# A gated linear attention feeding a gated MLP on one core: a shorter weight conversion, a third engine for v's copies, and a new table of due times

## The chip, the cores and the metric

The kernel runs on one core of a Trainium2 chip. The metric is device time in microseconds, the median over several executions of the program. One core has five engines with a queue of instructions each: TensorE (PE in the profile, with its weight loads as PEld), VectorE (DVE), ScalarE (ACT), GpSimd (POOL) and SyncE (SP), which here issues all DMAs.

## The reference

```python
# attention: batch 4, heads 8, sequence 768, head size 48
f = 1.0 / (1.0 + np.exp(-f_logit))
for t in range(S):
    state = f[:, :, t, :, None] * state + einsum('bhd,bhe->bhde', k[:, :, t], v[:, :, t])
    y[:, :, t] = einsum('bhd,bhde->bhe', q[:, :, t], state)
x = y.transpose(0, 2, 1, 3).reshape(B, S, H * D)          # 4 x 768 x 384
# MLP with a spatial gate: d_ff 1024, halves of 512
h = gelu_tanh(x @ w_in)
u, v = h[..., :512], h[..., 512:]
v_n = (v - mean(v)) / sqrt(var(v) + 1e-06) * g_ln
v_s = einsum('ts,bsd->btd', w_sg, v_n) + b_sg[None, :, None]
return x + (u * v_s) @ w_out
```

q, k, v, the gates, `w_sg` and the output are float32. `w_in` and `w_out` are float64: the kernel gets them as pairs of 32-bit words and turns them into float32 on the chip.

## The kernel before, in words

**Tiles.** Tokens go in 24 tiles n of 128 (six to a batch; tiles 0 to 5 are batch 0). Attention works on chunks of 64 tokens, two to a tile. The MLP works on groups g of three tiles, with four slices ft of 128 features.

**Two-word products.** The MLP's matmuls run on pairs "hi" and "lo" in a rounded float32 format, three matmuls to a product (`mm3`, L691), so every operand is split: ScalarE writes hi as a cast, VectorE writes lo as the difference.

**Steps.** The program is a list of named steps. For tile n:

- `f`, `k`, `q`, `v`: loads on SP. `w{n}.0`, `w{n}.1`: copies of half of v's heads to the other 64 partitions.
- `e`, `l` (exp, ln on ScalarE), then `cum` (matmul), then `up`, `dn` (exp on ScalarE), `mq`, `mk` (products); for tiles from 6 on, `lh`, `ll` split the logarithm ahead of `cum`.
- `tr` and `tc` turn k and q on PE for tiles 0 to 5. For the others it goes over DRAM: `tt` (VectorE transposes 32x32 blocks), `to` and `ti` (DMA out to `kq_d` and back into `raw`), `tc` (copy).
- `su` (scores and state updates, 128 small matmuls), `ms` (mask), `sa`, `sm` (state), `y` (128 small matmuls), `ty` (ScalarE), `jy` (VectorE), `xT` (three PE transposes), `xh`, `xl` (split).
- `hv` (MLP's v half), `gv` (gelu on ScalarE), `ns`, `nd`, `nq`, `nr`, `nh`, `nl` (the norm; `nr` on POOL).
- For group g: `hu`, `gu` (u half), `sg` (spatial gate, 18 matmuls each, after all six `nl` of the batch), `sb`, `sm_`, `sh`, `sl` (gate and split), `po` for each tile (projection), `re` (residual), `out` (store).

The weights go through `ld`, `wa` to `wf`: eight pieces `in0` to `in7` of w_in (0 to 3 for `hu`, 4 to 7 for `hv`) and four `out0` to `out3` of w_out; `ldsg`, `wT`, `wh`, `wl` do w_sg. In the kernel before a piece takes one ScalarE pass (`wa`), then `wb`, `wp`, `wq`, `wr`, `wc` on VectorE, `wd` and `wf` on VectorE or POOL, `we` on ScalarE.

**The order** is neither the source's nor the hardware's. `Plan` runs a list scheduling over the steps with costs from the table `T` (microseconds by engine) and `W` (SP's issue and the wire), due times worked back from the PE units, four PSUM banks, and rings of buffers (`gg` 5, `u` 8, `tmp` 3, `f` 4 and so on). Where `T` names several engines for a step, the planner picks one. `MOVES` shifts the due time of single steps and pins some to an engine. What comes out is written to the engines' queues as it stands, and each engine works its queue in order. Before 45 us of plan time, `warm` puts matmuls on zeros (L1044) wherever the plan leaves PE free. ScalarE keeps one table of functions: exp and ln are in one, gelu in the other, and each change between them is an ACT_TABLE_LOAD (L318).

A second path for gates out of range stands behind the main one and does not run with these inputs.

Of the kernel before, what the change touches and what calls it, by code (L numbers as in the profile page):

```python
# [66 lines left out]
wbin0:388.1 wdin0:-42.7:POOL wcin1:371.6 wrin3:343.8 wcin3:-99.1 wdin3:305.4:DVE wdin4:86.5 wfin4:224.6:DVE wrin5:88.5  # L67
wbin6:70.5 wfin6:-0.5:POOL wbin7:342.5 wrin7:222.5 wfin7:136.9:POOL ldout0:43.3 wfout0:-139 ldout1:444.3
wdout1:136.6:POOL wfout2:61.6 waout3:53.5 wbout3:-15.3 wT0.0:91.5 wh0.1:-323.2 wh1.0:110.6 ldsg2:2 wT2.1:74.4
wT3.0:32.3 wT3.1:232.8 wh4.0:7.4 ldsg5:32.4 mk0:0:DVE gv0:144.9 sm1.0:199.8:DVE xl1:61.2 v2:144.4 mk2:12 sa2.0:-2.5  # L70
sm2.0:340.9:DVE hu0.0:375.7 sm_0.0:-69.3:POOL sh0.0:-10.7 gu0.1:-79.4 sh0.1:-351.3 sm_0.2:73.7:DVE sg0.3:8.6
sm_0.3:-17.5:POOL po2:3.4 q3:27.8 w3.0:279.8:POOL w3.1:134.8 mq3:18.2:POOL di3:0:ACT tr3:227.2 sa3.0:169.8
sm3.0:-36.7:POOL xT3:264 w4.0:31.8:DVE sm4.0:0:POOL sm4.1:-12.4:POOL di5:-1.7:ACT sa5.0:15.5 nq5:-64.4 sg1.0:60.2
hu1.1:-126.3 gu1.1:75.2 gu1.2:304 sg1.2:-16.5 sm_1.3:-21.7:POOL sh1.3:13.3 sl1.3:-78.5 w6.1:493.6 ll6:0:DVE
tt6.0:229.6 tc6.0:23:ACT jy6:-75.7 xh6:-10.7 hv6:871.9 w7.0:-989.6:DVE w7.1:12.5:DVE ll7:0:DVE up7:128.7 mq7:-20.5:DVE
tt7.0:-318.4 re7:0.4 l8:57.9 cum8:383.5 mq8:-15.5:POOL mk8:-82.7:POOL ti8.3:80.5 tc8.1:6.9:DVE w9.0:0.2 mq9:70.4:POOL
su9:-124.4 xh9:304.7 k10:3.4 w10.1:-0.7:POOL e10:94.9 ll10:0:POOL mq10:-57.5:POOL mk10:99.2:DVE ti10.0:58.9 y10:78.5
k11:-124.5 lh11:66.2:ACT ll11:-2.8 mq11:2.7:POOL sg3.0:97.1 sg3.1:1.3 gu3.3:322.4 sg3.3:226.2 lh12:1.3:DVE up12:-79.1
tc12.0:-7.4:ACT nh12:-0.2 nl12:70.3 w13.0:75.3 w13.1:15.3 lh13:-59.7:ACT tc13.0:-224.1:ACT tc13.1:28.3 sm13.0:132.2
nq13:46.6 v14:14.3 tc14.1:-0.4:DVE hu4.1:161 sm_4.1:0:POOL f15:1.4 lh15:97.8:DVE ll15:29:POOL mq15:26.2:DVE  # L80
tc15.0:-201.2:DVE sm15.1:0.4:POOL f16:46.8 cum16:-214.9 ti16.2:-27.6 sm16.0:14 lh17:-144.9:DVE tc17.1:0:DVE sg5.1:84.7
up18:-24.4 mq18:-24.2:POOL tt18.1:-11 tc18.0:2.9 hv18:176.5 ll19:44.9 mq19:61.5 mk19:63.2:POOL sm19.1:-76 ll20:3.7
tc20.1:75.1:ACT hu6.1:185.8 sm_6.2:-119.2 sg6.3:95.4 sm_6.3:62.9 k21:-26.5 lh21:279.1:ACT tc21.0:-3.3 w22.0:-80.9
w22.1:148.4:POOL lh22:0:DVE tc22.0:36:DVE tc22.1:0.9 sm22.0:-85.9:DVE sm22.1:200.1:DVE w23.1:24.1:POOL ll23:81.9:POOL
mk23:85.3 sm23.0:0:POOL
# [210 lines left out]
def gla_moe_kernel(ctx: ExitStack, tc: tile.TileContext, q, k, v, f, w_in, g_ln, w_sg, b_sg, w_out, cst, out):  # L296
    nc = tc.nc
# [97 lines left out]
    def w_abs(key):  # L395

        w = staged[key].rearrange("p (n x) -> p n x", x=2)
        t = [buf("u", [P, E], U32, j) for j in range(2)]
        nc.scalar.activation(t[0].bitcast(F32), w[:, :, 1].bitcast(F32), AF.Abs)
        w_tmp[key] = (w, *t)  # L400

    def w_scale(key):
        _, a, _ = w_tmp[key]
        nc.vector.tensor_scalar(a.bitcast(F32), a.bitcast(F32), F32_LEAST, 2.0**16, op0=ALU.max, op1=ALU.mult)

    def w_shift(key):
        _, a, _ = w_tmp[key]
        nc.vector.tensor_scalar(a, a, 4, 1, op0=ALU.logical_shift_left, op1=ALU.logical_shift_right)
# [752 lines left out]
```

## Time and profile before

| | |
|---|---|
| median of 3 runs | 380.57 us (379.48 to 382.3) |
| the profiled execution | 379.31 us; its span, first to last instruction, 377.5 us |
| PE busy | 359.7 us, 95% of the span |
| DVE, ACT, POOL busy | 250.7, 244.7, 51.9 us |
| matmuls on zeros (L1044) | 14.8 us of PE |
| ACT_TABLE_LOAD | 36 (35 on L318, one on L300), 1283 ns each |
| mean granted PE clock | 0.992 of full |

PE's busy time holds the matmuls on zeros. Steps named above are found in the profile by line and tile: `hv`, `hu`, `sg`, `po` are all L691 and differ in their operands, `su` is L619 and L624, `y` L667, `xT` L696, `wb` L404, `wp` L408, v's copies and others L325.

### The profile page before, as it was taken

To read this page: it belongs to the slowest core of one execution; us is meant where nothing else is said; L and a number is where in the kernel's file an instruction comes from. 1 tells how busy PE (TensorE), PEld (TensorE's weight loads), DVE (VectorE), ACT (ScalarE), POOL (GpSimd) and SP (SyncE) were. 2 spreads that over 40 slices of the span, in tenths; PEclk is the share of its full clock that TensorE was granted. 3 is DMA by queue.
4 is the path that set the end of the run, shared out by engine and by line. 5 is a ranking of instruction groups with operands and counts; after the bars stand their busy time and mean duration, and the time that the engine had idled before them with its cause. 6 is when DMAs were issued, how large, how long until landed. Compare 5 with 4: busy or idle time off the path is not lost.

```text
span 377.5 us, 11316 instructions
## 1 busy us (share of the span) xinstructions
PE 359.7 (95%) x4662; PEld 324.7 (86%) x4662; DVE 250.7 (66%) x588; ACT 244.7 (65%) x507; POOL 51.9 (14%) x95
## 2 busy tenths in 40 slices
PE   8998999899999998799999999999999999999993
...
PEclk9999999999999999899999999999999999999998
...
GB/s 165 245 205 231 207 209 244 175 86 128 44 168 148 131 170 175 161 195 179 135 160 116 0 65 172 169 190 112 36 43 119 104 55 25 2 0 0 3 63 69
DMA packets 145998, 46.30 MB, mean 123 GB/s; under 512 B 117524, under 2 KB 144532, under 8 KB 145940
## 3 DMA queue, kind: packets, MB, share of 16 engines
...
HBM read 33.64 MB, written 11.85 MB: 121 GB/s over the span
## 4 chain that ended last, share of the span: by engine, by line
PE 55%; ACT 18%; DMA 10%; DVE 8%; SPq 3%; issue 3%; POOL 1%; ACTq 0%
PE ps_b L691 40%; ACT L318 5%; PE ps_b L1044 4%; PE ps_y L667 3%; DMA raw<-kq_d 3%; ACT vg L320 2%; ACT sk L325 2%; SPq L599 2%; DMA f<-in_f_logit_dram 2%; ACT f L320 2%; ACT vg L733 2%; ACT vh L746 2%; PE ps_s L619 2%; PE ps_b L521 1%; DMA kq<-in_q_dram 1%
## 5 line engine op out<-in xcount | busy, mean ns | idle before, releaser
L691 PE MATMUL ps_b<-w_sg_hi,vh 128*128 128x384 f32 x192 | 65.7, 342 | 0.0
L691 PE MATMUL ps_b<-w_sg_lo,vh 128*128 128x384 f32 x192 | 64.8, 338 | 0.0
L691 PE MATMUL ps_b<-w_sg_hi,vh_lo 128*128 128x384 f32 x192 | 64.8, 338 | 0.0
L691 PE MATMUL ps_b<-w_out_hi,gg 128*128 128x384 f32 x174 | 48.1, 339 | 0.4 <-ACT f L320 0.4
L318 ACT ACT_TABLE_LOAD x35 | 44.9, 1283 | 0.6
L794 ACT CAST gg<-tmp 128x384 fp32r<-128x384 f32 x29 | 14.8, 511 | 43.8 <-DVE tmp L783 37.7
L691 PEld LDWEIGHTS ps_b<-w_sg_hi,vh 128*128 128x128 f32 x192 | 36.0, 188 | 0.6 <-DVE w_sg_lo L939 0.2
L691 PEld LDWEIGHTS ps_b<-w_sg_lo,vh 128*128 128x128 f32 x192 | 36.1, 188 | 0.1
L691 PEld LDWEIGHTS ps_b<-w_sg_hi,vh_lo 128*128 128x128 f32 x192 | 36.0, 188 | 0.0
L320 ACT ACTIVATE f<-f 128x384 f32<-128x384 f32 x48 | 24.6, 522 | 12.9 <-DMA f<-in_f_logit_dram 12.6
L691 PEld LDWEIGHTS ps_b<-w_out_hi,gg 128*128 128x128 f32 x174 | 31.7, 188 | 1.0 <-ACT f L320 0.8
L691 PE MATMUL ps_b<-xTh,w_in_hi 128*128 128x384 f32 x84 | 29.3, 348 | 1.8 <-ACT vg L320 1.7
L778 DVE SCALAR_TENSOR_TENSOR tmp<-ps_b,cols,b_bc 128x384 f32<-128x384 f32 x32 | 19.6, 612 | 17.0 <-PE ps_b L691 17.0
L667 PEld LDWEIGHTS ps_y<-vs,st 64*64 64x64 f32 x768 | 24.7, 134 | 6.5 <-issue 5.2
L751 DVE SCALAR_TENSOR_TENSOR vh_lo<-vg,vg_rs,vh 128x512 fp32r<-128x512 f32 x24 | 18.0, 749 | 17.4 <-ACT vh L746 17.3
L691 PE MATMUL ps_b<-w_out_lo,gg 128*128 128x384 f32 x87 | 29.1, 335 | 0.0
L667 PE MATMUL ps_y<-S,sk 48*64 48x48 f32 x768 | 27.4, 220 | 1.2 <-issue 1.2
L691 PE MATMUL ps_b<-xTl,w_in_hi 128*128 128x384 f32 x84 | 28.4, 338 | 0.0
L691 PE MATMUL ps_b<-xTh,w_in_lo 128*128 128x384 f32 x84 | 28.4, 338 | 0.0
L691 PE MATMUL ps_b<-w_in_hi,xTh 128*128 128x512 f32 x63 | 26.9, 427 | 0.9 <-DVE xTl L716 0.9
L667 PE MATMUL ps_y<-vs,st 64*64 64x48 f32 x768 | 27.7, 220 | 0.0
L619 PE MATMUL ps_s<-sk 48*64 48x64 f32 x768 | 24.1, 231 | 1.9 <-ACT sk L325 1.9
...
## 6 DMA issues: line engine op xcount, KB each, us to landing
...
```

The lines of the kernel that those rows point to most:

```text
L318: nc.scalar.preload_act_table_set(SETS[want])
L320: nc.scalar.activation(dst, src, func, **kw)
L325: (nc.scalar.copy if e == "ACT" else ENG[e].tensor_copy)(dst, src)
L599: ENG[e].dma_start(raw[row : row + r1 - r0].rearrange("d b a t -> d b (a t)"), kq_d[n, :, r0:r1, m].rearrange("b r j y -> r b (j y)"))
L619: nc.tensor.matmul(ps_s[rows(score_rows(c, 2 * p + par)), par, p * C : (p + 1) * C], sk[r, 0, p, c], sk[r, 1, p, c], start=True, stop=True)
L667: nc.tensor.matmul(ps_y[rows(c), half, h * D : (h + 1) * D], a, m, start=start, stop=stop)
L691: nc.tensor.matmul(ps, a, m, start=(j == 0), stop=(j == len(seq) - 1))
L733: nc.scalar.activation(v_raw[n], v_raw[n], AF.Identity, bias=v_st[n][0][:, 0:1])
L751: nc.vector.scalar_tensor_tensor(vl, v_raw.pop(n), rs, vh.bitcast(F32), op0=ALU.mult, op1=ALU.subtract)
L778: nc.vector.scalar_tensor_tensor(t, psum[f"sg{g}.{ft}"][:, :E], g_col[:, ft : ft + 1], b_bc[:, tokens(g)], op0=ALU.mult, op1=ALU.add)
L794: nc.scalar.copy(gt[(g, ft)][0], g_raw[(g, ft)])
L1044: steps = plan.warm(plan.run(), 45.0, lambda k, n: nc.tensor.matmul(ps_b[k][:, : n * P], zeros, zeros[:, None, :].to_broadcast((P, n, P)), ...
```

## The change

**The conversion.** A piece loses one VectorE pass. Before, `wb` clamped and scaled the absolute value and `wp` shifted it left by four and right by one; now the scaling is the `scale` of ScalarE's `wa`, which was an Abs without one, and `wp` shifts left by three alone. `wb` is gone, twelve instructions in all.

**v's copies** may now go on ScalarE too. The plan puts 5 of the 48 there, 6 on POOL and 37 on VectorE; before it was 6 on POOL and 42 on VectorE.

**The table of moves** is another one, found with step times that were disturbed at random. It moves steps on every engine.

```diff
-F32_LEAST = float(np.uint32(0x38100000).view(np.float32))
+EXP_DOWN = 2.0**-112
...
-    ok_e="DVE:0.25", w="DVE:0.267 POOL:0.45", wT=0.25, ...
+    ok_e="DVE:0.25", w="DVE:0.267 POOL:0.45 ACT:0.33", wT=0.25, ...
...
 MOVES = """
-wbin0:388.1 wdin0:-42.7:POOL wcin1:371.6 wrin3:343.8 ...
+cs:-38.3 wain0:-74.5 wdin0:8.6:POOL ldin1:-40.4 wfin1:-79.9:POOL ...
...
-        nc.scalar.activation(t[0].bitcast(F32), w[:, :, 1].bitcast(F32), AF.Abs)
+        nc.scalar.activation(t[0].bitcast(F32), w[:, :, 1].bitcast(F32), AF.Abs, scale=EXP_DOWN)
         w_tmp[key] = (w, *t)
-
-    def w_scale(key):
-        _, a, _ = w_tmp[key]
-        nc.vector.tensor_scalar(a.bitcast(F32), a.bitcast(F32), F32_LEAST, 2.0**16, op0=ALU.max, op1=ALU.mult)
 
     def w_shift(key):
         _, a, _ = w_tmp[key]
-        nc.vector.tensor_scalar(a, a, 4, 1, op0=ALU.logical_shift_left, op1=ALU.logical_shift_right)
+        nc.vector.tensor_scalar(a, a, 3, None, op0=ALU.logical_shift_left)
...
-            op("wb" + s, lambda e, key=key: w_scale(key), T["wb"], ["wa" + s], port=True)
-            op("wp" + s, lambda e, key=key: w_shift(key), T["wp"], ["wb" + s], port=True)
+            op("wp" + s, lambda e, key=key: w_shift(key), T["wp"], ["wa" + s], port=True)
```

**Where steps move.** The lines of the kernel after the change are three or four lower than those of before (L691 becomes L688, L1044 becomes L1040). Three places follow.

The head of SP's queue before (gate logits `f`, the constants `cs`, q and k of tile 0 in `kq_90`, v, then four pieces of w_in):

```order
L480 DMA f<-in_f_logit_dram 128x8x48
L911 DMA cs<-in_consts_dram 128x320
L480 DMA f<-in_f_logit_dram 128x8x48
L483 DMA kq_90<-in_q_dram 128x8x48
L483 DMA kq_90<-in_k_dram 128x8x48
L486 DMA vs_93<-in_v_dram 128x8x48
L483 DMA kq_91<-in_q_dram 128x8x48
L390 DMA gg<-in_moe_w_in_dram 128x3x256 x4
L483 DMA kq_91<-in_k_dram 128x8x48
L480 DMA f<-in_f_logit_dram 128x8x48
```

The same place now:

```order
L382 DMA gg<-in_moe_w_out_dram 128x768
L477 DMA f<-in_f_logit_dram 128x8x48
L908 DMA cs<-in_consts_dram 128x320
L480 DMA kq_90<-in_q_dram 128x8x48
L391 DMA gg<-in_moe_w_in_dram 128x3x256
L480 DMA kq_90<-in_k_dram 128x8x48
L477 DMA f<-in_f_logit_dram 128x8x48
L483 DMA vs_93<-in_v_dram 128x8x48
L480 DMA kq_91<-in_q_dram 128x8x48
L391 DMA gg<-in_moe_w_in_dram 128x3x256
L480 DMA kq_91<-in_k_dram 128x8x48
L391 DMA gg<-in_moe_w_in_dram 128x3x256 x3
```

Two pieces of weights, `out3` and `in1`, have moved ahead of the first tile's operands; they were the 58th and the 29th transfer of the queue before. All that stands behind them up to the third `f` has two transfers of weights more ahead of it.

ScalarE's queue from the table load ahead of the first gelu, `gv0`, before (the gelu writes `vg`; `sk` and `w_sg_hi_80` are copies out of PSUM, `w_in_hi` a split):

```order
L318 ACT_TABLE_LOAD
L320 ACTIVATE vg,vg_mv<-ps_b_69 128x512
L325 COPY sk_96<-ps_b_68 112x512
L325 COPY sk_96<-ps_b_67 112x512
L671 COPY x<-ps_y 128x384
L712 CAST w_sg_hi_80<-ps_b_69 128x3x128
L320 ACTIVATE vg,vg_mv<-ps_b_70 128x512
L938 CAST w_sg_hi_79<-ps_b_67 128x3x128
L325 CAST w_in_hi_75<-u 128x3x128
L733 ACTIVATE vg<-vg,vg_mv 128x512 x2
L738 ACTIVATE vh_lo,vg_mv<-vg 128x512 x2
```

The same place now:

```order
L319 ACT_TABLE_LOAD
L321 ACTIVATE vg,vg_mv<-ps_b_67 128x512
L326 COPY sk_97<-ps_b_70 112x512
L400 ACTIVATE u<-gg 128x384
L730 ACTIVATE vg<-vg,vg_mv 128x512
L326 COPY dec<-ps_b_68 112x4x2
L735 ACTIVATE vh_lo,vg_mv<-vg 128x512
L709 CAST w_sg_hi_80<-ps_b_67 128x3x128
L934 CAST w_sg_hi_79<-ps_b_68 128x3x128
L319 ACT_TABLE_LOAD
L321 ACTIVATE eb_103<-ps_b_69 128x8x48
L668 COPY x<-ps_y 128x384
```

`gv0` has come forward, with fewer steps ahead of it, and the table goes back to exp (for `eb`, step `up5`) eight instructions later; before, the second gelu came without a table load in between. Over the whole main path the table loads become 44, from 36.

PE's queue between `y10` and `y11` (tiles 10 and 11, L667 here, L664 after) before: the end of `y10`, `cum15` (two matmuls on lh and ll), `xT10`, and the start of `y11`:

```order
L667 MATMUL ps_y<-vs_94,st 64x48
L667 MATMUL ps_y<-S_100,sk_96 64x48
L524 MATMUL ps_b_68<-lh,cum 128x384
L525 MATMUL ps_b_68<-ll,cum 128x384
L696 MATMUL ps_b_67<-cs,x 128x128 x3
L667 MATMUL ps_y<-vs_95,st 64x48 x2
L667 MATMUL ps_y<-S_101,sk_97 64x48 x3
```

Now `y10` is followed by `su11`, `hu2.3` and `po4`, and then by this: `xT10`, the nine rows of `po5`, `xT9`, the first matmul of `cum15`, with `y11` behind it.

```order
L693 MATMUL ps_b_70<-cs,x 128x128 x3
L688 MATMUL ps_b_69<-w_out_hi,gg 128x384
L688 MATMUL ps_b_69<-w_out_lo,gg 128x384
L688 MATMUL ps_b_69<-w_out_hi,gg 128x384 x2
L688 MATMUL ps_b_69<-w_out_lo,gg 128x384
L688 MATMUL ps_b_69<-w_out_hi,gg 128x384 x2
L688 MATMUL ps_b_69<-w_out_lo,gg 128x384
L688 MATMUL ps_b_69<-w_out_hi,gg 128x384 x2
L688 MATMUL ps_b_69<-w_out_lo,gg 128x384
L688 MATMUL ps_b_69<-w_out_hi,gg 128x384
L693 MATMUL ps_b_67<-cs,x 128x128 x3
L521 MATMUL ps_b_68<-lh,cum 128x384
```

What stood directly behind one another, `y10`, its transposes and `y11`, now has `su11` and three large products in between.

More of the change, by code (lines that the diff above doesn't have):

```diff
@@ L47 @@
     nl="DVE:0.663", gu="ACT:0.38", sb="DVE:0.534", sm_="DVE:0.468 POOL:1.05", sh="ACT:0.402", sl="DVE:0.467", re="DVE:0.467", ok="DVE:1.2",
-    ok_e="DVE:0.25", w="DVE:0.267 POOL:0.45", wT=0.25, cumf=0.72, cum=0.352, do=0.716, tr=0.791, tt="DVE:0.48", zr="POOL:2.2", tr_c="ACT:0.49 DVE:0.46", su=0.83, y=0.905, xT=0.25, hv=2.094, hu=1.584,
+    ok_e="DVE:0.25", w="DVE:0.267 POOL:0.45 ACT:0.33", wT=0.25, cumf=0.72, cum=0.352, do=0.716, tr=0.791, tt="DVE:0.48", zr="POOL:2.2", tr_c="ACT:0.49 DVE:0.46", su=0.83, y=0.905, xT=0.25, hv=2.094, hu=1.584,
     sg=3.167, po=2.084, ok_s=0.12,
@@ L66 @@
 MOVES = """
[L67 to L85, printed above, removed]
+cs:-38.3 wain0:-74.5 wdin0:8.6:POOL ldin1:-40.4 wfin1:-79.9:POOL wpin2:49.7 wcin2:13.8 wrin3:268.2 wein3:40.6
+ldin4:-0.6 wpin4:-54.8 wdin4:102.7:DVE wfin4:0:POOL wcin5:-123 wrin6:1.1 wdin6:-11.9:POOL wqin7:11.9 wfin7:94.1
```

20 lines of the change are left out of this document (19 added, 1 removed).

## The prediction

> **What bounds the kernel now.** First the page's shares, the slices of PE and its clock, and the chain that ended last.
>
> ```profile
> span 377.5 us, 11316 instructions
> PE 359.7 (95%) x4662; PEld 324.7 (86%) x4662; DVE 250.7 (66%) x588; ACT 244.7 (65%) x507; POOL 51.9 (14%) x95
> PE   8998999899999998799999999999999999999993
> PEclk9999999999999999899999999999999999999998
> PE 55%; ACT 18%; DMA 10%; DVE 8%; SPq 3%; issue 3%; POOL 1%; ACTq 0%
> ```
>
> PE is busy nearly all the time, so what can be won is where it is not busy, where its clock is low, and where it only works on zeros. The busy times by stretch show the places (columns: length, busy us and instructions of PE, PEld, DVE, ACT, POOL, then PE's clock, the DMA share, GB/s).
>
> ```profile
> 0.00:42.50 42.50, 40.23 (x599) 28.23 (x600) 32.87 (x88) 29.19 (x67) 7.51 (x18) 1.00 1.03 209
> 42.50:76.40 33.90, 31.40 (x452) 27.55 (x450) 28.67 (x72) 33.58 (x75) 9.59 (x18) 1.00 0.89 206
> 76.40:120.00 43.60, 43.00 (x477) 40.66 (x476) 37.38 (x82) 29.83 (x63) 9.19 (x9) 1.00 0.49 118
> 120.00:150.00 30.00, 28.34 (x513) 25.15 (x515) 21.33 (x51) 25.83 (x53) 4.59 (x8) 1.00 0.69 156
> 150.00:156.00 6.00, 3.35 (x126) 2.46 (x121) 4.04 (x9) 5.44 (x11) 1.20 (x2) 1.00 0.70 152
> 156.00:160.00 4.00, 4.00 (x71) 3.43 (x68) 2.51 (x7) 0.15 (x1) 0.00 (x0) 0.57 0.84 148
> 160.00:190.00 30.00, 29.48 (x505) 26.32 (x503) 22.49 (x55) 29.33 (x58) 3.71 (x7) 1.00 0.83 170
> 190.00:370.00 180.00, 178.29 (x1944) 169.70 (x1944) 100.77 (x227) 91.37 (x184) 16.15 (x33) 1.00 0.31 75
> 370.00:377.50 7.50, 1.57 (x10) 1.25 (x8) 0.64 (x2) 0.00 (x0) 0.00 (x0) 0.81 0.17 58
> ```
>
> Length less PE's busy time gives the idle time: 2.27 us to 42.5, 2.50 to 76.4, 0.60 to 120, 1.66 to 150, 2.65 in the six microseconds from 150, nothing to 160, 0.52 to 190, 1.71 to 370, and 5.93 at the end, when the last result goes out. At 0.57 of its clock, the four microseconds to 160 held 2.28 us of work: another 1.72 us lost. A last part hides in "busy":
>
> ```profile
> L1044 PE MATMUL ps_b<-zeros 128*128 128x512 f32 (+3 forms) x32 | 14.8, 589 | 1.0 <-DVE zeros L1046 1.0
> ```
>
> These 14.8 us on zeros lie in the first 45 us, where the plan had nothing for PE. So there are **two places to win**: the front to 120, with 14.8 us of zeros and 5.4 us of waits; and the rest to 370, with 4.83 + 1.71 us of waits and 1.72 us of low clock, 8.3 us in all.
>
> What ends the front is ScalarE. It is busy 33.58 of the 33.9 us between its first gelu and `nh5`, the last norm that the first spatial gate (`sg`) needs; the DMA engines are full as well (share 1.03, then 0.89).
>
> ```profile
> 42.52 0.60 ACT L320 ACTIVATE vg<-ps_b 128x512 f32<-128x512 f32 x1
> 75.66 0.73 ACT L746 ACTIVATE vh<-vg,vg_rs 128x512 fp32r<-128x512 f32 x1
> 77.60 0.44 PE L691 MATMUL ps_b<-w_sg_hi,vh 128*128 128x384 f32 x1
> ```
>
> `gv0` starts at 42.52, `nh5` ends at 76.39, the first `sg` starts 1.21 us later.
>
> **The change part by part.** *One VectorE pass fewer.* Rows of the passes, of v's copy, and of the nearest forms on ScalarE:
>
> ```profile
> L404 DVE TENSOR_SCALAR u<-u 128x384 f32<-128x384 f32 x12 | 4.2, 353 | 0.0
> L408 DVE TENSOR_SCALAR u<-u 128x384 uint32<-128x384 uint32 x12 | 4.6, 381 | 0.1
> L399 ACT ACTIVATE u<-gg 128x384 f32<-128x384 f32 x12 | 6.7, 558 | 2.5 <-DMA gg<-in_moe_w_in_dram 2.5
> L325 DVE COPY vs<-vs 64x192 f32<-64x192 f32 x42 | 11.1, 264 | 4.3 <-DMA vs<-in_v_dram 3.2
> L733 ACT ACTIVATE vg<-vg,vg_mv 128x512 f32<-128x512 f32 x24 | 17.3, 725 | 1.7 <-DVE vg_mv L730 1.7
> L671 ACT COPY x<-ps_y 128x384 f32<-128x384 f32 x24 | 11.6, 482 | 5.9 <-PE ps_y L667 5.3 <-DVE u L412 0.5
> L325 ACT COPY dec<-ps_b 112x8 f32<-112x8 f32 x2 | 0.4, 177 | 1.1 <-PE ps_b L558 1.1
> ```
>
> `wb` takes 12 x 353 ns = 4.2 us off VectorE. `wp` keeps its form with one operand less: between 353 ns (L404, same size) and its present 381; I keep 381. `wa` gets a scale: 558 ns as now is one end; the other is the 725 ns of the wider `nd` (L733), which has an operand more, hence at most 12 x 0.17 = 2 us on ScalarE; I keep 558. Five copies of v go from VectorE (5 x 264 ns = 1.3 us) to ScalarE, where such a copy isn't in the trace. Above it lies a copy of twice the width, `ty` (L671) with 482 ns, below it `di` (`dec`) with 177 ns; I take 0.35, so 1.8 us, with 0.9 and 2.4 as ends. VectorE thus sheds 5.5 us, of which three `mq` and three `sm_` that leave POOL for it take some back. None of that goes to the end directly: ScalarE and DMA end the front, and behind 120 VectorE is idle a third of the time. Its worth is that `jy`, `xl` and `wf` come sooner, some tenths at a time.
>
> *The front, rearranged.* SP now fetches `out3` and `in1` first. Three pieces of w_in arriving in a row show the price of such a transfer while the queue is full:
>
> ```profile
> 11.09 0.58 ACT L399 ACTIVATE u<-gg 128x384 f32<-128x384 f32 x1 [0.64 <-DMA gg<-in_moe_w_in_dram]
> 12.21 0.56 ACT L399 ACTIVATE u<-gg 128x384 f32<-128x384 f32 x1 [0.54 <-DMA gg<-in_moe_w_in_dram]
> 13.34 0.57 ACT L399 ACTIVATE u<-gg 128x384 f32<-128x384 f32 x1 [0.57 <-DMA gg<-in_moe_w_in_dram]
> ```
>
> They are 1.12 us apart, so the loads behind those two come 2.2 us later, those behind `in1`'s old place 1.1 us. Tile 0's attention waits for that, and the plan pays with zeros: 8448 columns in 23 matmuls now, 6656 in 16 before (the sums of the widths in PE's order). One row prices them:
>
> ```profile
> 14.30 2.84 PE L1044 MATMUL ps_b<-zeros 128*128 128x512 f32 x6
> ```
>
> Three matmuls of 512 columns (six records) took 2.84 us, 1.85 ns a column; 1792 columns more are **+3.3 us** of zeros, in time that PE would otherwise idle. Against that, two conversions now fall into the first microseconds, where VectorE waits, and `hv0` stands 6.2 us of PE work earlier (behind `tr2`, no longer behind `tr3`, `su2`, `y2` and `su3`). `gv0` then starts near 33 to 35 us by PE's own queue: five `cum`, three `do`, three `tr`, two `su`, two `y`, one `xT` and two `wT` ahead of `hv0`, at 0.45, 0.79, 0.9, 0.99, 1.08, 0.25 and 0.42 us from start to start, are 12.6 us; zeros 18.1, the start 1.05, `hv0` itself 2.2. From `gv0` to `nh5` ScalarE then has more to do than before: 73 steps for 56 (six `wa`, four `e`, three `l` among them), and two more table loads. Summed by the start-to-start times of each kind before, that is 42.5 us after, 32.8 before (33.9 measured). Scaled alike, 43.9 us: `nh5` ends at 77 to 79 and `sg` starts at 78 to 80, against 77.6. But `hu1.3`, 1.67 us of PE, is now done ahead of it, so the front comes out **at 0 us**, with -1.5 to +2.5 as ends.
>
> *The table loads.*
>
> ```profile
> L318 ACT ACT_TABLE_LOAD x35 | 44.9, 1283 | 0.6
> ```
>
> 44 instead of 36 are 8 x 1.283 = **10.3 us more on ScalarE**. Two are in the 43.9 us above. Two more lie between `gv6` and `gv11`, where ScalarE has 29.33 of 30 us busy (160 to 190); four lie behind, where it is busy 91 of 180 us, and that idle time hides them. I take 0 for those six here and leave the price to a rival.
>
> *The waits behind 120.* The largest stand around `y10` to `su12` (first three rows; below them the groups of the steps in between):
>
> ```profile
> 151.77 0.44 PE L525 MATMUL ps_b<-ll,cum 128*128 128x384 f32 x1 [0.64 <-POOL ll L512]
> 153.10 0.55 PE L696 MATMUL ps_b<-cs,x 128*128 128x128 f32 x3 [0.89 <-DVE x L675]
> 155.82 0.34 PE L619 MATMUL ps_s<-sk 48*64 48x64 f32 x8 [1.10 <-ACT sk L325]
> 134.96 0.55 PE L696 MATMUL ps_b<-cs,x 128*128 128x128 f32 x3 [0.72 <-DVE x L675]
> 146.01 0.55 PE L696 MATMUL ps_b<-cs,x 128*128 128x128 f32 x3 [0.93 <-ACT vg L320]
> L675 DVE SCALAR_TENSOR_TENSOR x<-ps_y,x 128x384 f32<-128x384 f32 x24 | 13.2, 550 | 4.9 <-ACT x L671 4.5
> L712 ACT CAST xTh<-ps_b 128x384 fp32r<-128x384 f32 x21 | 10.0, 476 | 12.0 <-PE ps_b L696 9.7 <-PE ps_b L691 2.1
> L716 DVE TENSOR_TENSOR xTl<-ps_b,xTh 128x384 fp32r<-128x384 f32 x21 | 11.6, 551 | 4.2 <-ACT xTh L712 4.1
> ```
>
> `cum15` waited for `ll15` on POOL, `xT10` for `jy10`, `su12` for the copy `tc12.1`. After the change `ll15` is on VectorE, and `su11`, `hu2.3` and `po4` stand between `y10` and `xT10`: 1.0 + 1.7 + 2.1 = 4.8 us of work over `ty10` and `jy10`, which need 0.48 + 0.55 us (L671, L675) and their latencies. `su12` comes behind `po5` and `y11` besides. So all 2.65 us there go, and with them the 1.72 us of low clock, which set in right after: **-4.4 us**. Of the other 2.18 us between 120 and 190, I give half: `xT8` has `cum14` and `po3` ahead of it (2.6 us) where it had `po5` (2.1), hardly better, and `xT9` waited for a PSUM bank, which the new order places elsewhere: **-1.1 us**. Of the 1.71 us behind 190, a third: **-0.6 us**. Against this stand tight places that the new order makes: `hv7` to `po3` and `su10`, where ScalarE's work from `gv7` to `tc10.1` fills 5.3 of 6.0 us of PE work, and `xT18` to `hv18`, where `xh` and `xl` (0.48 + 0.55 us) have only `y19` (1.1 us) to hide behind. Nothing to 4 us; **+1.3 us**, about one wait of the size above.
>
> [...]
>
> **The sum**: 0 - 4.4 - 1.1 - 0.6 + 1.3 = -4.8 us. On the profiled execution's 379.31 us that is 374.5. Its time lies 1.26 us under the median shown, 380.57, so the median should come to **375.8 us**.
>
> **Rivals.**
>
> *The waits only move* (379 to 384, middle 380.6). Each gap above is a step that came less than a microsecond late in a dense order. If the new order, as dense, has as many such places, the 6.1 us come back elsewhere. For it: the tight places named, and a ScalarE with 10.3 us more to do. Against: large products now stand where `y` followed `y`.
>
> *ScalarE becomes the bound* (385 to 390, slower). Place: from `hv2` to `hv5` and from `gv7` to `nh11`. ScalarE's work there grows by four table loads, 5.1 us, and by weights and exps drawn forward; it decides if `gv0` comes later than 36 us, or if ScalarE idles over 13 us between the first `sg` and `su10`. Each microsecond later is one on the end: 3 us in front and 4 behind, with no gain, give 387. For it: 29.33 of 30 us busy at 160 to 190. Against: ScalarE is busy only 29.83 of 43.6 us from 76.4 to 120, where work drawn forward fits. [...]
>
> *The front shrinks as well* (367 to 372). If VectorE, 5.5 us lighter, was what held `hv0` and the tiles behind it, `gv0` comes by 31 us, and 3 to 4 us more go. Against it: DMA share 1.03 to 42.5 us, and more zeros in the plan.
>
> *The new passes don't shorten VectorE*: if `wp` or `wa` ran slower than now, at most 2 us; inside the forecast's own range.
>
> **Chances.** Forecast 0.52 (372 to 379.5), waits only move 0.25, ScalarE the bound 0.09, front shrinks 0.14. Leaving out the slower rival and the outermost part of the front's gain, 370.5 to 383.0 holds 8 in 10; the forecast's ends are the front's 4 us and the new waits' 4 us. A measurement of this kernel tells about 1% from no change: under 376.8 is faster, over 384.4 slower. Under 376.8 fall 0.37 of the forecast's 0.52 and all of the last: 0.51. Over 384.4 falls ScalarE's 0.09. Between them lies 0.40.
>
> **What would show it.** Right: no L404 of 353 ns, L408 near 381, DVE busy near 245 us, 44 table loads and ACT near 257 us, zeros near 18 us; `gv0` at 33 to 35, the first `sg` at 78 to 80; PE idle between 120 and 190 under 3.5 us with no slice of PEclk below 9 there. Wrong: `sg` beyond 82 (ScalarE or the loads held the front), or idle time of 5 us or more between 120 and 370 with other releasers (the waits moved), or a low clock at a new place.

## The result and the profile after

The changed kernel takes **375.97 us** (median; 374.96 to 376.25) against 380.85 us before in the same session: a ratio of 0.9861, 95% interval 0.9816 to 0.9906. In a second session, beside the experiments below, it was 375.54 us, ratio 0.9825 (0.9785 to 0.9865). The forecast was 375.8 us. The profiled execution took 376.25 us, its span is 374.4 us.

First the page of the changed kernel: its shares, the clock's slices, the chain that ended last, and the table loads.

```profile
span 374.4 us, 11350 instructions
PE 360.0 (96%) x4676; PEld 326.9 (87%) x4676; DVE 248.0 (66%) x574; ACT 258.9 (69%) x519; POOL 47.2 (13%) x93
PEclk9999999999999999999999999999999999999998
PE 60%; ACT 16%; DVE 8%; DMA 6%; SPq 4%; issue 3%; POOL 0%; ACTq 0%; DVEq 0%
...
L319 ACT ACT_TABLE_LOAD x43 | 55.2, 1283 | 0.8
```

PE's busy time is as before; the span is 3.1 us shorter because PE idles less. No slice of the clock is below 9 but the last, which is 8 as it was before, when only the end of the program is left. With the load at L301 that opens the kernel there are the 44 table loads foreseen. The stretches, cut as they were for the kernel before (length, busy us and count of PE, PEld, DVE, ACT, POOL, then PE's clock, DMA share, GB/s):

```profile
0.00:42.50 42.50, 39.66 (x596) 28.38 (x597) 32.79 (x80) 31.10 (x69) 10.47 (x22) 1.00 1.03 220
42.50:76.40 33.90, 31.74 (x450) 27.09 (x449) 29.75 (x76) 33.45 (x74) 8.78 (x16) 1.00 0.85 188
76.40:120.00 43.60, 43.13 (x537) 40.99 (x537) 35.88 (x78) 34.73 (x68) 4.90 (x6) 1.00 0.49 114
120.00:150.00 30.00, 29.27 (x494) 27.02 (x492) 22.09 (x53) 25.27 (x52) 5.50 (x11) 1.00 0.77 174
150.00:156.00 6.00, 5.42 (x148) 4.83 (x147) 3.06 (x8) 5.94 (x11) 0.00 (x0) 1.00 1.05 214
156.00:160.00 4.00, 4.00 (x20) 3.26 (x19) 3.94 (x11) 3.94 (x9) 0.00 (x0) 1.00 0.52 130
160.00:190.00 30.00, 29.84 (x392) 27.45 (x392) 19.94 (x49) 25.41 (x53) 2.33 (x6) 1.00 0.73 144
190.00:368.00 178.00, 176.84 (x2051) 167.88 (x2049) 99.99 (x224) 99.05 (x190) 15.21 (x32) 1.00 0.33 79
```

Length less PE's busy time, from 120 to 190 us: 0.73 + 0.58 + 0 + 0.16 = 1.47 us, where it was 4.83; behind 190 it is 1.16 us for 1.71; and the 0.57 of clock at 156 to 160 us is 1.00. The front went the other way. Two steps of ScalarE and one of PE mark it, `gv0`, the end of `nh5` and the first `sg`:

```profile
35.80 0.60 ACT L321 ACTIVATE vg<-ps_b 128x512 f32<-128x512 f32 x1
79.75 0.75 ACT L743 ACTIVATE vh<-vg,vg_rs 128x512 fp32r<-128x512 f32 x1
83.15 0.44 PE L688 MATMUL ps_b<-w_sg_hi,vh 128*128 128x384 f32 x1 [0.47 <-ACT f L321]
```

Since the steps stand in another order, times of one step can't be set side by side. What can be is **the lag**: a step's start less the PE work that stands ahead of it in the queue, each step counted at its kind's usual time from start to start (`hv` 2.19 us, `hu` 1.67, `sg` 3.17, `po` 2.11, `y` 1.08, `su` 0.99, `tr` 0.9, `do` 0.79, `cum` 0.45, `wT` 0.42, `xT` 0.25), zeros not counted. A lag that grows shows time lost to waits, zeros or a low clock. Read from the traces at steps with that much work ahead of them, in us:

| kernel | 10 | 75 | 119 | 144 | 190 | 335 | of it, lost at half clock |
|---|---|---|---|---|---|---|---|
| before | 15.9 | 22.8 | 23.5 | 30.1 | 30.2 | 31.6 | 1.7, between 119 and 144 |
| changed | 19.6 | 25.6 | 26.1 | 27.2 | 27.1 | 28.1 | 0 |
| changed, second session | 19.4 | 27.5 | 27.7 | 28.3 | 28.8 | 29.4 | 1.7, before 75 |
| conv_alone | 15.7 | 22.4 | 23.8 | 29.9 | 29.9 | 33.3 | 1.7, between 119 and 144 |
| order_alone | 21.1 | 30.1 | 30.6 | 30.7 | 30.4 | 32.7 | 3.4, before 75 |
| tc4_early | 19.5 | 25.1 | 25.7 | 25.7 | 25.6 | 26.1 | 0 |

The changed kernel is 2.8 us behind at the end of the front, and wins 5.5 us between 119 and 144: there the kernel before lost 6.6 us, the changed one 1.1.

### The profile page after: what moved, and what is told of

Same layout as the page of the kernel before. It is cut to its first block, busy times and chain, and to the rows that moved or that the text cites. A ratio compares the mean times of both kernels' runs of the same rounds, so it can differ in the third digit from the quotient of the medians.

```text
span 374.4 us, 11350 instructions
## 1 busy us (share of the span) xinstructions
PE 360.0 (96%) x4676; PEld 326.9 (87%) x4676; DVE 248.0 (66%) x574; ACT 258.9 (69%) x519; POOL 47.2 (13%) x93
## 4 chain that ended last, share of the span: by engine, by line
PE 60%; ACT 16%; DVE 8%; DMA 6%; SPq 4%; issue 3%; POOL 0%; ACTq 0%; DVEq 0%
PE ps_b L688 48%; ACT L319 4%; PE ps_y L664 3%; PE ps_b L1040 2%; DMA kq<-in_q_dram 2%; PE ps_s L616 2%; DMA raw<-kq_d 2%; ACT sk L326 2%; ACT vh L743 2%; SPq L596 2%; ACT f L321 1%; ACT vh_lo L735 1%; ACT vg L321 1%; ACT vg L730 1%; PE ps_s L621 1%
## 5 line engine op out<-in xcount | busy, mean ns | idle before, releaser
L688 PE MATMUL ps_b<-w_sg_hi,vh 128*128 128x384 f32 x192 | 65.8, 343 | 0.5 <-ACT f L321 0.5
L688 PE MATMUL ps_b<-w_sg_hi,vh_lo 128*128 128x384 f32 x192 | 64.9, 338 | 0.0
L688 PE MATMUL ps_b<-w_sg_lo,vh 128*128 128x384 f32 x192 | 64.8, 338 | 0.0
L688 PE MATMUL ps_b<-w_out_hi,gg 128*128 128x384 f32 x174 | 47.8, 338 | 0.0
L688 PEld LDWEIGHTS ps_b<-w_sg_hi,vh 128*128 128x128 f32 x192 | 36.0, 188 | 1.6 <-ACT f L321 0.8
L688 PEld LDWEIGHTS ps_b<-w_sg_lo,vh 128*128 128x128 f32 x192 | 36.1, 188 | 0.1
L688 PEld LDWEIGHTS ps_b<-w_sg_hi,vh_lo 128*128 128x128 f32 x192 | 36.0, 188 | 0.0
L791 ACT CAST gg<-tmp 128x384 fp32r<-128x384 f32 x29 | 14.9, 512 | 28.8 <-DVE tmp L780 28.5
L775 DVE SCALAR_TENSOR_TENSOR tmp<-ps_b,cols,b_bc 128x384 f32<-128x384 f32 x32 | 19.6, 612 | 20.3 <-PE ps_b L688 20.2
L688 PEld LDWEIGHTS ps_b<-w_out_hi,gg 128*128 128x128 f32 x174 | 31.7, 188 | 0.1
L688 PE MATMUL ps_b<-xTh,w_in_hi 128*128 128x384 f32 x84 | 29.2, 348 | 1.2 <-ACT vg L321 1.2
L664 PEld LDWEIGHTS ps_y<-vs,st 64*64 64x64 f32 x768 | 24.6, 134 | 6.2 <-issue 2.5
L664 PE MATMUL ps_y<-vs,st 64*64 64x48 f32 x768 | 27.4, 220 | 1.8 <-DVE st L626 1.8
L688 PE MATMUL ps_b<-w_out_lo,gg 128*128 128x384 f32 x87 | 29.1, 335 | 0.0
L321 ACT ACTIVATE f<-f 128x384 f32<-128x384 f32 x48 | 25.1, 528 | 4.9 <-DMA f<-in_f_logit_dram 4.1
L688 PE MATMUL ps_b<-xTl,w_in_hi 128*128 128x384 f32 x84 | 28.5, 339 | 0.0
L688 PE MATMUL ps_b<-xTh,w_in_lo 128*128 128x384 f32 x84 | 28.4, 338 | 0.0
L664 PE MATMUL ps_y<-S,sk 48*64 48x48 f32 x768 | 27.2, 220 | 0.0
L688 PE MATMUL ps_b<-w_in_hi,xTh 128*128 128x512 f32 x63 | 26.1, 415 | 0.7 <-DVE xTl L713 0.7
L688 PE MATMUL ps_b<-w_in_hi,xTl 128*128 128x512 f32 x63 | 24.9, 395 | 0.0
L688 PE MATMUL ps_b<-w_in_lo,xTh 128*128 128x512 f32 x63 | 24.8, 393 | 0.0
```

The source lines that it names most:

```text
L321: nc.scalar.activation(dst, src, func, **kw)
L664: nc.tensor.matmul(ps_y[rows(c), half, h * D : (h + 1) * D], a, m, start=start, stop=stop)
L688: nc.tensor.matmul(ps, a, m, start=(j == 0), stop=(j == len(seq) - 1))
L775: nc.vector.scalar_tensor_tensor(t, psum[f"sg{g}.{ft}"][:, :E], g_col[:, ft : ft + 1], b_bc[:, tokens(g)], op0=ALU.mult, op1=ALU.add)
L791: nc.scalar.copy(gt[(g, ft)][0], g_raw[(g, ft)])
```

## The experiments

All times are medians; a ratio is to the kernel before on the same chip, and not exactly the quotient of the medians. The kernel before had 381.63 us beside experiments 1 and 2, 381.28 us beside experiment 3 and `v_on_vector`, and 382.83 us beside experiment 4 and `loads_twice`.

**1. Order and conversion apart.** `order_alone` is the new order with the old two passes; `conv_alone` the old order with the new conversion.

```
order_alone:  AF.Abs)                                     # no scale
              tensor_scalar(a, a, F32_LEAST, 2.0**16, op0=max, op1=mult)
              tensor_scalar(a, a, 4, 1, op0=shift_left, op1=shift_right)
conv_alone:   AF.Abs, scale=EXP_DOWN)                     # w_scale: pass
              tensor_scalar(a, a, 3, None, op0=shift_left)
```

Expected of the yardstick: 

> The changed kernel once more, as the yardstick beside which the next three are read: 375 to 376.3 us, 4 to 5 us under the kernel before.

Expected of `order_alone`: 

> The new order of steps with the old conversion: VectorE scales and shifts in two passes again, 12 more passes of 0.353 us, 4.2 us. Theory (the gain is the order's: what stands where on TensorE): 375.5 to 377 us, at most 1 us over the changed kernel, since VectorE idles a third of the time and the front ends on ScalarE. Rival (the lighter VectorE is what lets the weights and jy come sooner, as the change's words suggest): 378 to 380.5 us, most of the gain gone.

Expected of `conv_alone`: 

> The old order of steps with the new conversion: the scaling pass is dropped from VectorE and nothing takes its place, ScalarE scales in its own pass. Theory (the order): 379.8 to 381 us, as before. Rival (the lighter VectorE): 376 to 378.5 us.

Measured: the changed kernel 375.54 us, 0.9825 (0.9785 to 0.9865); `order_alone` 379.11 us, 0.9916 (0.9882 to 0.9950); `conv_alone` 381.04 us, 0.9986 (0.9957 to 1.0015). The conversion alone does nothing that can be told, the order alone about half of the gain, both together 3 us more than the sum of the two. For `order_alone` the rival's range was met, not the theory's. Its trace shows the first place where the pass counts. These are the matmul on zeros ahead of `su1`, and `xl0` on VectorE, whose PSUM bank those zeros use; first of `order_alone`, then of the changed kernel:

```profile
23.48 0.49 PE L1041 MATMUL ps_b<-zeros 128*128 128x128 f32 x2 [1.01 <-DVE w_sg_hi L714]
...
22.88 0.54 DVE L714 TENSOR_TENSOR w_sg_hi<-ps_b,w_sg_hi 128x384 fp32r<-128x384 f32 x1
```

```profile
22.07 0.38 PE L1040 MATMUL ps_b<-zeros 128*128 128x128 f32 x2
...
21.01 0.55 DVE L713 TENSOR_TENSOR w_sg_hi<-ps_b,w_sg_hi 128x384 fp32r<-128x384 f32 x1
```

In the new order the conversions of out3, in1 and in4 to in7 share VectorE's queue with tiles 0 and 1. The scaling passes of 0.35 to 0.38 us there bring `xl0` 1.87 us later; the zeros wait 1.01 us for its bank, with PE's whole queue behind them, and the lag at 10 is 21.1 us for 19.6. In the old order taking these passes out brought nothing that can be told (`conv_alone`). So the two parts of the change are not independent: the order was made for the lighter VectorE. Of the rest, the lag of `order_alone` at 75 contains 3.4 us of low clock, that of the changed kernel 0 in one profile and 1.7 in the other.

Between 119 and 144 the table parts the two changes: the lag of `order_alone` grows by 0.1 us there and that of the changed kernel by 1.1, those of `conv_alone` and of the kernel before by 6.1 and 6.6. The gain in that stretch is the order's, with either conversion.

**2. Zeros taken out.** `fewer_zeros` drops the four matmuls on zeros ahead of `tr2` and `tr4`.

```
-    steps = plan.warm(plan.run(), 45.0, ...
+    steps = plan.warm(plan.run(), 27.0, ...
```

> The changed kernel without the four matmuls on zeros ahead of tr2 and tr4 (1664 columns, 2.8 us in its trace). Theory (these zeros run on after the step behind them is ready: tr2's last input was done at 29.24 us and it started at 32.35, tr4's at 42.28 and it started at 45.77): 373 to 374.5 us, and zeros of about 17 us. Rival (a PSUM bank or ScalarE holds those steps anyway, the zeros only fill the wait): 375.5 to 376.5 us, with the wait in the place of the zeros.

Measured: 376.72 us, 0.9837 (0.9794 to 0.9879), no gain. `tr4` starts at 43.88 us, 1.89 earlier, and `xT2` no earlier (48.12 us for 47.99): it needs the bank that `tc4` empties. Timeline of PE and ScalarE in this run:

```profile
48.12 0.43 PE L693 MATMUL ps_b<-cs,x 128*128 128x128 f32 x1 [3.20 <-ACT sk L326]
...
46.66 0.51 ACT L326 CAST w_in_hi<-u 128x384 fp32r<-128x384 f32 x1 [0.15 <-POOL u L422]
47.07 0.52 ACT L321 ACTIVATE f<-f 128x384 f32<-128x384 f32 x1
47.50 1.05 ACT L326 COPY sk<-ps_b 112x512 f32<-112x512 f32 x2
```

The two `tc4` copies (last row) stand behind `e7`, `wein0` and `l7` on ScalarE. The rival's mechanism was right, though the time lies 0.2 us above its range: the zeros only filled a wait. In this profile the pause of 3.20 us left bare was followed by 6.8 us at half clock (experiment 4).

**3. Three moves of single steps.** `tc4_early` acts on what the last run showed, `e8_later` on ScalarE's table loads, `old_hv9_early` on the largest term of the prediction, in the kernel before.

```
tc4_early:      no zeros ahead of tr4; behind it in the list:
                sm3.1 ll6 tc4.0 tc4.1 xT2 ms3 e7 do4 xh2 wein0 wfin0 w4.1 y3
                l7 xl2 wpin2 di4 su4 gv1 mq5 wqin2 mk5
e8_later:       e8 behind e10
old_hv9_early:  hv9 and xT10 swap banks; xh9 behind lh15; xl9 behind y10;
                hv9 behind sm11.0; up14 behind ty10;
                tc12.0 tc12.1 up15 dn15 xh10 xl10 behind y11
```

> The changed kernel without the two matmuls on zeros ahead of tr4, and with tc4 and xh2 ahead of e7, wein0 and l7 on ScalarE, ms3 ahead of nl0's followers on VectorE. Theory (zeros and ScalarE's queue are one wait: tr4's copy stood behind e7, wein0 and l7, so taking the zeros alone gave nothing): xT2 starts at 46 us for 48, hv2 at 50 to 51 for 52.5, no pause of over 1.5 us and so no low clock, 373 to 374.5 us. Rival (VectorE, busy 29.8 of 33.9 us there, holds y4 anyway): 375 to 376 us.

> The changed kernel with one step moved: e8 stood alone between two gelus (52 to 56 us) and now follows e10, which spares two table loads, 2.57 us of ScalarE, 41 loads for 43. Theory (ScalarE, without a pause from 46 to 80 us in the changed kernel, sets what TensorE waits for there): the 0.84 us ahead of hv3 and the 0.72 us ahead of the first sg go, 373.9 to 374.6 us, 1 to 1.6 us under the changed kernel. Rival (table loads are hidden there too, VectorE holds the tiles): 375.2 to 376 us.

> The kernel before, with one place of its order changed by hand: hv9, 2.2 us of large products, moves ahead of cum15 and so into the waits around y10 (it and xT10 swap PSUM banks, xh9 moves ahead of up14 and its table load, xl9 to the end of y10, tc12 ahead of up15). Theory (the prediction's largest term: 2.65 us of waits there and the 1.72 us of low clock that follow): most of it goes, 376.5 to 378.5 us, and no low clock at 156 to 160. Rival (the waits only move, since su12 waits for a transfer that lands at 154.6 us and ScalarE is busy throughout): 380 to 382 us.

Measured: `tc4_early` 373.70 us (372.88 to 374.42), 0.9799 (0.9764 to 0.9833); `e8_later` 376.10 us, 0.9863 (0.9817 to 0.9909); `old_hv9_early` 381.53 us, 1.0000 (0.9973 to 1.0026).

`tc4_early` came out where its theory said, but not wholly by its steps. `xT2` starts at 46.23 us; then `tr5` waits for `mk5` on VectorE, so that `hv2` starts at 52.07 and not at 50 to 51:

```profile
46.23 0.33 PE L693 MATMUL ps_b<-cs,x 128*128 128x128 f32 x1 [1.18 <-ACT sk L326]
...
51.23 0.32 PE L570 MATMUL ps_b<-cs,kq 128*112 128x128 f32 x1 [1.03 <-DVE kq L535]
```

Its longest wait of PE is 1.44 us, and its profile has no fall of the clock. That the one follows from the other, as the theory had it, is not shown: the fall in `e8_later` came with no wait over 1.2 us in the 3.5 us ahead of it.

By the table 0.5 us are won in the front, 1.0 more by 144, and another 0.5 behind. Nothing was moved there; why the later part gains is not settled.

`e8_later` has two table loads fewer in the stretch where ScalarE is busiest (33.45 of the 33.9 us from 42.5 us on in the changed kernel), and no gain that shows: the waits ahead of `hv3` (0.79 us, for `xl3` on VectorE) and of the first `sg` (0.32 us) stay. Its profile has 3.41 us at half clock from 49.95 us on, up to 1.7 us lost, which the changed kernel's first profile has not; this can hide a gain. Whether ScalarE, busy without a pause, is the bound of that stretch is not settled by this run.

`old_hv9_early` filled the wait behind `y10` and got it back one place on. PE waits for `jy11`, which follows four other steps on VectorE behind `xl10`, and `xl10` waits for `xh10`, which the edit itself had put behind `tc12`, `up15` and `dn15` on ScalarE; the first of these, the two copies of `tc12` (last row), wait for a transfer:

```profile
160.38 0.47 PE L696 MATMUL ps_b<-cs,x 128*128 128x128 f32 x1 [2.87 <-DVE x L675]
...
157.54 0.56 DVE L716 TENSOR_TENSOR xTl<-ps_b,xTh 128x384 fp32r<-128x384 f32 x1 [3.95 <-ACT xTh L712]
...
159.76 0.56 DVE L675 SCALAR_TENSOR_TENSOR x<-ps_y,x 128x384 f32<-128x384 f32 x1
...
155.23 1.14 ACT L325 COPY sk<-raw 112x512 f32<-112x512 f32 x2 [1.21 <-DMA raw<-kq_d]
```

The rival's number was met. The transfer it named has a part in it, but the long wait stands at `xT11` (first row) and not at `su12`. The clock fell here too, for 6.83 us where the kernel before has 3.41. In this placing one large product of 2.2 us is not cover enough. The new order puts `su11`, `hu2.3`, `po4` and `po5` there, 6.9 us, and has one wait of 0.58 us left. That other placings of `hv9` alone would gain nothing is not shown.

**4. The clock.** Stretches at half clock ahead of the last microseconds occur in ten of the 14 profiles. The rows below are pairs, the 3.5 us ahead of a fall and the fall itself: of the kernel before, of the changed kernel's second profile, of `order_alone` and of `fewer_zeros`.

```profile
152.60:156.10 3.50, 1.90 (x87) 1.61 (x88) 1.47 (x4) 2.95 (x7) 0.00 (x0) 1.00 0.79 169
156.10:159.60 3.50, 3.50 (x67) 3.01 (x58) 2.11 (x5) 0.05 (x1) 0.00 (x0) 0.51 0.82 139
```

```profile
26.80:30.30 3.50, 1.84 (x69) 1.59 (x69) 3.46 (x7) 3.24 (x9) 1.81 (x2) 1.00 1.02 176
30.30:33.80 3.50, 3.50 (x9) 1.80 (x9) 2.92 (x8) 2.36 (x7) 0.33 (x1) 0.51 0.94 301
```

```profile
47.50:51.00 3.50, 1.99 (x18) 1.56 (x16) 3.47 (x6) 2.79 (x7) 2.51 (x2) 1.00 0.87 171
51.00:57.90 6.90, 6.41 (x143) 6.14 (x143) 5.68 (x17) 5.56 (x11) 0.92 (x2) 0.51 0.79 173
```

```profile
44.70:48.20 3.50, 0.30 (x3) 0.09 (x2) 3.47 (x8) 3.35 (x10) 1.70 (x1) 1.00 0.99 242
48.20:55.10 6.90, 6.90 (x146) 6.75 (x147) 4.57 (x14) 5.60 (x11) 1.74 (x3) 0.51 0.93 170
```

PE is busy 1.90, 1.84, 1.99 and 0.30 of the 3.5 us ahead. The first profile of the changed kernel has the same two places with nearly the same shares, and the clock holds:

```profile
27.00:30.50 3.50, 1.94 (x69) 1.60 (x69) 3.43 (x7) 3.24 (x10) 1.81 (x2) 1.00 0.89 148
30.50:34.00 3.50, 3.50 (x21) 2.58 (x20) 2.95 (x8) 3.24 (x10) 0.31 (x1) 1.00 0.98 322
46.50:50.00 3.50, 2.08 (x36) 1.57 (x36) 3.47 (x8) 3.44 (x6) 1.07 (x1) 1.00 0.84 127
```

`old_zeros` and `order_alone_zeros` put small matmuls on zeros into such pauses, the first in the kernel before around `y10`, the second in the new order with the old conversion; `tc4_zeros` does it in `tc4_early`.

```
+    one = lambda e: nc.tensor.matmul(ps_y[:, 0, E:512], zeros, zeros, ...)
old_zeros:                     3 ahead of cum15, 4 ahead of su12
order_alone_zeros, tc4_zeros:  5 ahead of y1, 4 ahead of xT2
```

> The kernel before with seven small matmuls on zeros (128 columns each, into columns of ps_y that nothing else uses) in its waits around y10: three ahead of cum15, four ahead of su12. No step is moved. Theory (the low clock after these waits comes of TensorE's idle share within a few microseconds, not of a long gap): the idle time there falls from 2.65 to about 1 us, the clock at 156 to 160 us stays at 1.00 and 1.7 us go, 379 to 380 us. Rival (the clock falls there for another reason, or only gaps count that are longer than any here): 381 to 382 us with the low clock as before.

> The new order with the old conversion, and small matmuls on zeros (128 columns each, into unused columns of ps_y) in its two largest pauses: five ahead of y1, four ahead of xT2. Theory (of the 3.6 us by which the new order with the old conversion stands behind the changed kernel about half is the clock that fell after those pauses, 3.2 us in its profile, the rest VectorE's 12 passes ahead of tile 0 to 2): 376.5 to 378 us, and runs within 2.5 us of each other where they lay 4.7 apart. Rival (it is all VectorE's passes): 378.5 to 379.5 us.

> The changed kernel with tc4 ahead and no zeros ahead of tr4 (as in tc4_early), and small matmuls on zeros in the pauses ahead of y1 (five) and xT2 (four). Theory (it is the fall of the clock after such pauses that parts one run from another): 372.8 to 373.6 us, runs within 1.5 us. Rival (the clock does not fall there once tc4 stands ahead, the zeros only delay): 373.7 to 374.5 us.

Measured: `old_zeros` 381.48 us, 0.9976 (0.9939 to 1.0013); `order_alone_zeros` 381.50 us, 0.9981 (0.9949 to 1.0013); `tc4_zeros` 378.23 us, 0.9894 (0.9849 to 0.9939). On the clock `old_zeros` did what its theory foresaw. Its stretches:

```profile
150.00:156.00 6.00, 5.11 (x189) 4.32 (x182) 4.48 (x9) 5.14 (x10) 1.20 (x2) 1.00 0.58 134
156.00:160.00 4.00, 3.28 (x78) 2.82 (x78) 0.73 (x2) 1.51 (x3) 0.00 (x0) 1.00 0.86 149
```

No step was moved, PE was only kept busier (5.11 of the six microseconds to 156, for 3.35 before), and the clock stayed at 1.00. Over its runs the mean granted clock was 0.996, against 0.986 for the kernel before beside it. The profile of `order_alone_zeros` has no fall either, but over its runs the clock was 0.993, the same as for `order_alone`. That it is the idle share that counts is the author's reading; no run parts it from other causes. On the time no gain can be told. In `old_zeros` PE now waits at full clock instead (0.72 us of the four to 160), because `su12` and `xT11` come no earlier; the interval runs from 0.6% faster to 0.1% slower, so the 1.7 us that the theory expected (0.45%) are neither shown nor ruled out. In the other two the zeros cost about 0.7 and 1 per cent, the ratios' differences from `order_alone` and `tc4_early`, which ran in other sessions. In `tc4_zeros` two new waits have nothing as their releaser but the issuing of instructions, and the clock falls at 52.7 us, where `tc4_early` has no fall:

```profile
43.84 0.39 PE L688 MATMUL ps_b<-w_in_lo,w_sg_hi 128*128 128x512 f32 x1 [0.57 <-issue]
50.95 0.24 PE L621 MATMUL ps_s<-vs,kq 64*48 64x48 f32 x2 [0.66 <-issue]
```

Where the rest of the cost comes from is not settled, and so the split of the 3 us between VectorE and the clock (experiment 1) stays open.

**5. The copies of v, and the table loads.** `v_on_vector` puts the five copies back on VectorE at the same places; `loads_twice` switches the table twice more ahead of nine gelu sections behind 190 us.

```
v_on_vector:  s["on"] = "DVE" for the w steps that are on "ACT"
loads_twice:  behind sg2.3, at each switch to gelu: load G, load E, load G
```

> The changed kernel with the five v copies that went to ScalarE (0.35 us each) back on VectorE, at the same places of the order. Theory (five copies of 0.25 to 0.35 us, at most one of them next to a wait): 375 to 376.3 us, as the changed kernel. Rival (w0.1, w2.1 and w4 stand on the chain of the first tiles, where VectorE is full): 376.5 to 378 us.

> The changed kernel with two table loads more ahead of each of the nine or so gelu sections behind 190 us, 2.57 us each and some 23 us more of ScalarE in all. Theory (behind 190 us ScalarE idles 79 of 178 us and its table loads are hidden): 375 to 377 us, at most 1.5 us over the changed kernel. Rival (a gelu that comes 2.57 us later holds its PSUM bank and the norms that the next gate waits for): each costs 0.5 us or more, 380 us and over.

Measured: `v_on_vector` 375.33 us, 0.9828 (0.9787 to 0.9868), as the changed kernel; `loads_twice` 393.31 us, 1.0301 (1.0244 to 1.0358). The eighteen loads more are 23.1 us of ScalarE, and the kernel is about 17 us longer; far outside the theory's range, as the rival had it. Stretches of the changed kernel, then of `loads_twice`:

```profile
220.00:250.00 30.00, 30.00 (x557) 27.29 (x559) 20.27 (x49) 28.12 (x51) 3.47 (x7) 1.00 0.80 175
250.00:285.00 35.00, 33.84 (x373) 32.44 (x365) 20.64 (x47) 22.33 (x40) 2.02 (x5) 1.00 0.43 97
285.00:368.00 83.00, 83.00 (x852) 79.27 (x850) 40.10 (x90) 30.95 (x66) 5.06 (x13) 1.00 0.11 33
```

```profile
220.00:250.00 30.00, 24.59 (x457) 20.62 (x457) 17.15 (x43) 28.61 (x41) 4.68 (x8) 1.00 0.68 149
250.00:285.00 35.00, 27.92 (x364) 24.54 (x363) 15.33 (x39) 33.12 (x55) 2.75 (x7) 0.90 0.43 90
285.00:368.00 83.00, 83.00 (x854) 79.48 (x853) 41.98 (x94) 39.52 (x76) 4.95 (x13) 1.00 0.12 35
```

Two thirds of ScalarE's idle time behind 190 us (52.1 of 79.0 us) lie in the last 83 us. Between 220 and 250 it is busy 28.12 of 30 us in the changed kernel, and with the loads added there the waits of PE in the first two stretches grow from 1.2 to 12.5 us. The clock falls there for 6.83 us as well (0.90 in the second row), 3.4 us more. In the last stretch, which holds three of the added loads, PE stays busy throughout.

## Why the prediction was right, point by point

**The total** was right (375.8 us for 375.97), and so was the reading that the largest gain lies around `y10`. That it was met to 0.2 us is in part luck. The two profiled executions differ by 3.1 us and not by the 4.8 of the sum: by the lag +2.6 up to 119, -5.5 up to 144, -0.2 up to 190, -0.4 up to 335 and +0.4 at the end. The medians differ by 4.9 us. The rest is in no term of the prediction. The profiled execution of the kernel before had a mean clock of 0.992, its runs beside experiment 1 had 0.987 (the changed kernel 0.997 in the profile, 0.996 over the six runs); 0.005 of 377.5 us is 1.9 us. By this estimate the usual run of the kernel before loses more to its clock than the one that was profiled.

**The waits behind 120**: forecast -4.4 - 1.1 = -5.5 us; the lag between 119 and 144 of work grows by 1.1 us for 6.6, a gain of 5.5. That this gain is the order's is shown by experiment 1. The reason given, large products between `y10` and `y11` as cover, fits the trace: `xT10` waits for nothing, and the one wait left there is that of `cum15` behind `xT9`, 0.58 us. No run takes the cover out of the new order, and one product moved in the old order did not bring the gain (`old_hv9_early`), so the cover as the cause is argued, not shown. Open too are the 1.72 us of low clock as a sum of its own: `old_zeros` took the low clock away and left the cover as it was, and no gain can be told.

**The front** at 0 us is the term that was mis-sized: the lag at 75 is 2.8 us larger, just over the worse end given (+2.5). `gv0` came at 35.80 us, not at 33 to 35, `nh5` ended at 80.50, not at 77 to 79, the first `sg` came at 83.15, not at 78 to 80; by its own mark, `sg` beyond 82, the front was held (its last 0.47 us were for `dn7`, which empties a PSUM bank, not for a norm). The zeros took 19.7 us from start to start (14.1 before), +5.6 where 3.3 was forecast, part of it waits that stand behind a matmul on zeros. The two transfers ahead of the first tiles cost what was said. `e2`, which needs the transfer of f2, starts 2.2 us later, before and after:

```profile
17.89 0.53 ACT L320 ACTIVATE f<-f 128x384 f32<-128x384 f32 x1
```

```profile
20.10 0.53 ACT L321 ACTIVATE f<-f 128x384 f32<-128x384 f32 x1 [0.63 <-DMA f<-in_f_logit_dram]
```

The lag is 1.9 us larger than before at `cum2`, which follows `e2`, and 1.3 us at `cum3`. At `y1` it is 3.6 us larger (19.55 for 15.92), and there PE waits for VectorE. The start of `y1` on PE and the mask `ms1` on VectorE that it needs, before and after:

```profile
27.50 0.26 PE L667 MATMUL ps_y<-vs,st 64*64 64x48 f32 x2
...
22.55 0.69 DVE L629 TENSOR_TENSOR st<-ps_s,cs 128x512 f32<-128x512 f32 x1
```

```profile
28.83 0.26 PE L664 MATMUL ps_y<-vs,st 64*64 64x48 f32 x2 [1.56 <-DVE st L626]
...
28.10 0.68 DVE L626 TENSOR_TENSOR st<-ps_s,cs 128x512 f32<-128x512 f32 x1
```

`su1` starts 2.1 us later than before, `ms1` 5.6 us later: VectorE works without a pause over 0.15 us from 13.89 us on, and five passes of weight conversions stand ahead of `ms1` after `su1` is done. So the step that failed is the one that gave VectorE no term in the front ("ScalarE and DMA end the front", the conversions falling where "VectorE waits"). That VectorE's load counts there is shown by `order_alone`, whose scaling passes raise the lag at 10 by 1.5 us. How the 2.8 us divide between the transfers, VectorE and what follows up to the first `sg` was read from the traces, not tried by a run.

**VectorE's pass** was to bring nothing directly. In the old order that is what `conv_alone` shows, as far as can be told; in the new order it is wrong, since taking the passes back costs 3.6 us there, an unknown part of it by the clock. The prices themselves held. Groups of the changed kernel by shape:

```profile
L400 ACT ACTIVATE u<-gg 128x384 f32<-128x384 f32 x12 | 6.8, 563 | 3.2 <-DMA gg<-in_moe_w_out_dram 2.0 <-DMA gg<-in_moe_w_in_dram 1.3
...
L405 DVE TENSOR_SCALAR u<-u 128x384 uint32<-128x384 uint32 x12 | 4.3, 361 | 4.1 <-ACT u L400 4.0
...
L326 ACT COPY vs<-vs 64x192 f32<-64x192 f32 x5 | 1.8, 351 | 1.6 <-DMA vs<-in_v_dram 1.5
```

`wa` with its scale takes 563 ns (558 assumed), `wp` 361 (between 353 and 381), a copy of v on ScalarE 351 (0.35 us), and where those copies run makes no difference that can be told. VectorE sheds less than foreseen, 248.0 us for 245.

**The table loads** at 0 us: no run takes out the eight that the change adds, so their price is open. The reason given was wrong: 91 busy of 180 us behind 190 is a mean over unlike stretches, in the changed kernel 28.12 of 30 us and 30.95 of 83. `loads_twice` shows 17 us for 23 there. The rival of ScalarE as the bound charged a microsecond for each one of ScalarE, where this run shows about 0.75, and it had the wrong place.

**New tight places**, +1.3 us, and -0.6 for the waits behind 190: behind 190 the lag grows by 1.0 us, 1.4 before, so 0.4 us are won where the two terms made a loss of 0.7. Of the two places named, `su10` waits 0.36 us and the other not at all. The largest wait, 1.17 us ahead of `hu5.3`, is for a gelu that stands directly behind a table load on ScalarE (250.14 to 251.42 us), so it may be a part of the loads' price.
